# A new table for the order and the engine of every operation in a one-core attention and gMLP kernel

## The chip, the cores and the metric

The kernel runs on one core of a Trainium2 chip (trn2). The metric is the device time of one execution in microseconds. A core has a matrix engine (TensorE, PE in the rows; its weight loads are PEld), VectorE (DVE), ScalarE (ACT), GpSimd (POOL) and a queue engine (SyncE, SP), on which this kernel issues nearly all its transfers. Each engine works through its own list of instructions in order. It stops where an instruction needs something that another engine or a transfer has not yet delivered, and all that stands behind that instruction on the same engine stops with it.

## The reference, cut to what matters

The input is q, k, v of 4 batches, 8 heads, 768 positions and 64 columns in float32, with the four weights of a gated MLP. Each query sees the keys less than 16 positions away and one summary key for each block of 32 positions (24 of them): the elementwise maximum of the block's keys, with the mean of the block's values as its value, and log(32) added to its score. The softmax runs over both kinds together. The heads side by side make x, 768 rows of 512 for each batch, and that goes through the MLP:

```python
h = np.maximum(x @ w_in, 0.0)            # 512 -> 1024
u, v = (h[..., :512], h[..., 512:])
v_n = (v - mean(v)) / np.sqrt(var(v) + 1e-06)
v_s = np.einsum('ts,bsd->btd', w_spatial, v_n) + b_spatial[None, :, None]   # mixes the 768 positions
return (u * v_s) @ w_out
```

## The kernel before, in words

**Recording and emitting.** The kernel is not written as loops that issue instructions. A first pass (`plan.add`, class `Plan`) records 2194 operations, each with the engines that may run it, a planned duration, the buffers that it reads and writes, and a function that issues its instructions. `Plan.order` then takes the operations one by one out of the table `ORDER`: three characters each, two for the operation's number in base 64 and one for the engine. For each it works out a planned start from fixed durations and assigns a slot to each of the operation's buffers that has none yet. The emission loop after that issues the operations sorted by planned start. So the table sets the order of the instructions on each engine, the engine of each operation that has a choice, and which slot each buffer gets and after whom. Two more things hang on the planned starts. The first is the filler: up to the operation "warm" TensorE gets one small matmul that nobody reads for each 300 ns of planned idle time (L904), 33 of them (two instructions each) before the first scores or weight preparation. The second is that a GpSimd operation planned in the first part of the kernel waits for the last VectorE operation on their common port that was emitted before it:

```python
listed = [(self.ops[LETTERS.index(ORDER[i]) * 64 + LETTERS.index(ORDER[i + 1])], ENGINES[int(ORDER[i + 2])]) for i in range(0, len(ORDER), 3)]
...
op, e = listed[len(made)] if listed else choose()
```

**Transfers.** All loads and stores but the last store are issued on SP's queue (helper `dma`, L267), in the table's order. A load into a slot waits on the queue until the slot's old content has been read, and the later loads wait behind it; no more than 8 transfers are outstanding at once. Buffers have few slots: one for a vT tile (`vt`), two alternating ones for the queries (qd) and for the values (ve), six for the spatial weights (`wl`) and three PSUM banks of the kind `m` for projections and other results.

**Names.** In the text `k0_1` is the load of the keys of batch 0, head pair 1; `q0_1_0` the load of the queries of batch 0, chunk 1 (256 positions), pair group 0; `v0_1_0` and `h0_1_0` the two loads of that group's values into ve; `vt1_0_2` the third quarter of batch 1's transposed values for head pair 0; `vn` the values of batch 0 in their natural layout; `wi1_c` and `wi0_c` the load of row block c of the v half and of the u half of w_in; `tr1_7_0` a reload of spatial weights for product 7 of batch 1, part 0.

**The start.** The weights must be split into a high part, which the matmul takes exactly, and a low part. For each block of w_in (`split64`, L283 to L320) ScalarE scales (L296), VectorE shifts and masks (L297, L298, L301, L305), one of the two casts (`copy`, L273), and TensorE or GpSimd forms the rest (L313 to L315, or L319 and L320). A key tile is prepared by VectorE's maxima over 16 keys (L400), a second maximum (L410) and ScalarE's copy into the key tile (L413). The "first scores" are those of batch 0, chunk 0, group 0, and need two key tiles and one query tile.

**Attention.** A group has 2 head pairs and 256 positions. TensorE computes its scores (s, L491) into PSUM; VectorE adds the mask and takes the maximum (L504), ScalarE exponentiates and sums (L508), VectorE adds a small constant and inverts the sums (L512, L514), and one of three engines normalizes (L519, L521). TensorE transposes (t, L540, L548), ScalarE or VectorE copies the result out as pt, and TensorE multiplies with the values ve (x, L564). x leaves PSUM as a high part xh (L273) and a low part xl (VectorE, L579). The block means of the values of batches 1 to 3 come from vT tiles that VectorE reduces (vs_in, L460).

**MLP.** Every product is three matmuls: high by high, and the two mixed ones (L598). proj v (pv) and proj u (pu) make the halves of h, with ReLU on the way out of PSUM; VectorE and others normalize v's rows (L630 to L646); the spatial products (sp) mix positions, VectorE adds them to sums and bias (L738, L740); a gate multiplies with u (L689), casts to gh (L273) and subtracts for gl (L691); proj out (po) gives the result, which leaves through a copy (ob) and a store. Batch 0 takes w_spatial as it is. For batches 1 to 3 w_spatial's quarters are combined beforehand into sums and differences, so that seven half-size products do for eight; these weights lie in device memory and are read back (tr, 384 KB each) into the six `wl` slots for each product. A reload can start as soon as the last product that reads its slot is done.

The attention of batch 0 (and a part of batch 1) comes first, with little projection work to lay beside it; from about 49 us TensorE has projections of one batch beside the attention of the next.

Of the kernel before, what the change touches and what calls it, by code (L numbers as in the profile page):

```python
# [197 lines left out]
def tile_local_summary_attention_gmlp(ctx: ExitStack, tc: tile.TileContext, qT, kext, vext, vnat, vT, w_in, w_sp, b_rep, w_out, out):  # L198
# [734 lines left out]
    "1P41Q21R11S11x41T11y21z11A11C21B10340810911G41H21I11J11D10240030510610100a21K11L21Y41Z20721+11-12012121E01F22210440b0"  # L933
    "0t10i10u20g10h20r10s20j20z40G30n10o21M10p10q20e10f21U10c10d21V12302410y40H30C40A40D40B40J00N20M20I30W40-10K20F3101112"
    "2O40k10l10V40v10w12P03510L22Q13622U12V22W12R21W02-10m32n42o20x30Y13312S13020Z10+20O00Q00R22p10P23112q12r13222s12u30X4"
    "1X21201711821912T20E41511621312e40S01422w41k11l21g11e12t12v31i11N03j43k05V40T10U11a21b11j25W11c11h26L01f21m11d13Q43a4"
    "1n12x22y11o12X23423712Y12f22g11O23813935X41p01q23n11r01s26z06A03y12543A12Z13B23l13o23w13x23p13C13D23r13e02F42+35Y12h1"
    "2i13z24l43m23s23E12z11t02k18q43q23t13F13G33R03W15Z43u11u23v31v12623b43c03d13f26M02G23H43I41w02j25+13Y13Z24716N02H1271"
    "3L02B12812I14512A12D33M24113X28Y43J03K28z43g03h26343U13i12a23S16O04316P26Q14m04E14622l33V24A14C13N03O26412m34D26R16S1"
    "4223P14c46B06T36C08n42J14824425-43T27702C17807902E14B28C44r16D24F22K13+17a04K42L18w46X08Z22M16Y06Z06+02917b22b14y14z2"  # L940
# [126 lines left out]
```

## Time and profile before

| | us |
|---|---|
| median of 3 runs (397.4 to 401.26) | 397.51 |
| the profiled execution | 399.03 |
| its span in the trace | 397.3 |
| TensorE busy | 380.5 |
| VectorE busy | 296.5 |
| ScalarE busy | 215.5 |
| GpSimd busy | 139.8 |

The mean granted clock of TensorE was 1.00 of full speed. In a row of a timeline the first number is the start within the span, the second the duration; the end of the row in square brackets is the idle time of the engine just before and what ended it. "issue" stands for no releaser that the profile shows. Matmuls are pipelined, so that the durations of neighbours overlap, and a row with a count groups instructions that follow one another.

### The profile page before, as it was taken

The page shows a single profiled execution, that of the slowest core. Times are in us where ns is not written, and L with a number is a line of the kernel's source. Part 1 is how long each engine was busy: PE and PEld are TensorE (multiplying, and loading weights), DVE is VectorE, ACT ScalarE, POOL GpSimd, SP SyncE. Part 2 cuts the span into 40 slices and gives each one's busy share as a digit, 9 for nine tenths or more (in the row PEclk, how much of TensorE's full clock was granted, in tenths as well). Part 3 has the DMA queues.
Part 4 walks back from the last instruction along what each step waited for, and adds up shares of the span by engine and source line. Part 5 has one row for each costly group of instructions (what it writes and reads, how often), then busy time and mean ns, then how long its engine had stood idle before and what let it go on. Part 6 is the DMA issues. An engine that isn't in the chain of part 4 may idle for free.

```text
span 397.3 us, 9692 instructions
## 1 busy us (share of the span) xinstructions
PE 380.5 (96%) x3523; PEld 331.5 (83%) x3523; DVE 296.5 (75%) x999; ACT 215.5 (54%) x703; POOL 139.8 (35%) x156
## 2 busy tenths in 40 slices
PE   8889798999999999997989999999999999999996
PEld 8667686899989888897978888899987888898985
DVE  4979798899998979978696586785697667463631
ACT  4779696588484684555448557265447482120110
POOL 4234406412345446661033034443441144310330
PEclk9999999999999999999999999999999999999999
DMA  7978789765366899798925696448961380059304
GB/s 284 395 187 241 193 274 259 217 205 167 133 199 231 298 266 309 240 296 297 357 91 170 197 330 159 127 121 267 298 209 24 105 272 7 2 184 316 148 1 159
DMA packets 41407, 81.77 MB, mean 206 GB/s; under 512 B 4496, under 2 KB 16272, under 8 KB 41360
## 3 DMA queue, kind: packets, MB, share of 16 engines
q1 hardware_dynamic: 41216, 81.02, 64.1%
q8 instruction: 28, 0.46, 0.5%
q14 instruction: 19, 0.16, 0.1%
q10 hardware_dynamic: 144, 0.13, 0.1%
HBM read 66.58 MB, written 14.55 MB: 204 GB/s over the span
## 4 chain that ended last, share of the span: by engine, by line
PE 76%; DVE 11%; DMA 8%; ACT 2%; issue 1%; SPq 1%; POOL 0%; ACTq 0%; DVEq 0%; POOLq 0%
PE sp L598 17%; PE pu L598 16%; PE pv L598 15%; PE po L598 15%; PE x L564 4%; PE s L491 3%; DVE p L504 3%; DMA tr<-mixed_w 3%; PE warm L904 3%; PE t L548 2%; DMA wi<-in_w_in_dram 2%; DMA wo<-in_w_out_dram 1%; DMA k<-in_kext_dram 1%; DVE gh L273 1%; DMA out_dram<-ob 1%
## 5 line engine op out<-in xcount | busy, mean ns | idle before, releaser
L508 ACT ACTIVATE p<-p,sums 128x120 f32<-128x120 f32 x192 | 73.8, 388 | 37.9 <-DVE sums L504 37.7
L504 DVE CUSTOM_DVE_ANT_0 p<-s,mask 128x120 f32<-128x120 f32 x192 | 44.9, 275 | 11.2 <-PE s L491 11.0
L598 PE MATMUL pu<-xh,win_h 128*128 128x512 f32 (+1 forms) x128 | 43.6, 341 | 0.0
L598 PE MATMUL pu<-xh,win_l 128*128 128x512 f32 (+1 forms) x128 | 43.1, 336 | 0.0
L598 PE MATMUL pu<-xl,win_h 128*128 128x512 f32 (+1 forms) x128 | 43.0, 336 | 0.0
L598 PE MATMUL po<-wo_h,gh 128*128 128x512 f32 (+1 forms) x100 | 38.8, 388 | 1.9 <-DVE xl L579 1.7
L598 PE MATMUL pv<-win_h,xh 128*128 128x512 f32 x96 | 38.8, 404 | 0.0
L598 PE MATMUL po<-wo_l,gh 128*128 128x512 f32 (+1 forms) x100 | 38.2, 382 | 0.0
L598 PE MATMUL po<-wo_h,gl 128*128 128x512 f32 (+1 forms) x100 | 38.2, 382 | 0.0
L598 PE MATMUL sp<-tr,vnh 128*128 128x384 f32 x144 | 37.6, 342 | 0.3 <-DMA tr<-mixed_w 0.2
L598 PE MATMUL pv<-win_l,xh 128*128 128x512 f32 x96 | 37.5, 391 | 0.0
L598 PE MATMUL pv<-win_h,xl 128*128 128x512 f32 x96 | 37.5, 390 | 0.0
L508 ACT ACTIVATION_READ_ACCUMULATOR p<-p,sums 128x1 f32 x192 | 36.5, 190 | 0.0
L277 ACT ACTIVATE u<-pu 128x384 f32<-128x384 f32 (+2 forms) x39 | 13.8, 379 | 41.7 <-PE pu L598 41.7
L598 PE MATMUL sp<-tr,vs 128*128 128x384 f32 x162 | 30.7, 339 | 2.1 <-DMA tr<-mixed_w 1.4
L519 ACT ACTIVATE p<-p,sums 128x120 f32<-128x120 f32 x92 | 28.2, 383 | 7.4 <-DVE sums L514 6.4
L521 POOL TENSOR_TENSOR p<-p,sums 128x480 f32<-128x480 f32 x16 | 15.7, 989 | 43.3 <-DVE sums L514 27.9
L598 PEld LDWEIGHTS sp<-tr,vs 128*128 128x128 f32 x162 | 27.8, 188 | 3.1 <-DVE sums L514 1.7
L564 PEld LDWEIGHTS x<-pt,ve 120*64 120x64 f32 x768 | 23.7, 138 | 7.8 <-issue 4.3
L564 PE MATMUL x<-pt,ve 120*64 120x64 f32 x768 | 25.7, 224 | 3.4 <-issue 1.6
L273 ACT COPY pt<-t 120x512 f32<-120x512 f32 x37 | 20.5, 589 | 12.1 <-PE t L548 9.9
L598 PEld LDWEIGHTS sp<-tr,vnh 128*128 128x128 f32 x144 | 25.3, 188 | 2.0 <-DMA tr<-mixed_w 0.9
(175 smaller groups left out, 931.8 us busy)
## 6 DMA issues: line engine op xcount, KB each, us to landing
tr<-mixed_w SPq DMA_DIRECT2D x36, 384.0 KB, 4.8
tr<-plain SPq DMA_DIRECT2D x27, 384.0 KB, 5.1
k<-in_kext_dram SPq DMA_DIRECT2D x16, 544.0 KB, 6.1
qd<-in_qT_dram SPq DMA_DIRECT2D x24, 256.0 KB, 4.3
ve<-in_vext_dram SPq DMA_DIRECT2D x23, 256.0 KB, 4.7
out_dram<-ob SPq DMA_DIRECT2D x23, 256.0 KB, 3.4
vt<-in_vT_dram SPq DMA_DIRECT2D x48, 96.0 KB, 2.7
wi<-in_w_in_dram SPq DMA_DIRECT2D x7, 512.0 KB, 6.8
```

The costliest lines, as they stand in the source:

```text
L273: (nc.scalar.copy if e == "ACT" else nc.vector.tensor_copy)(out=out_, in_=in_)
L277: nc.scalar.activation(out=out_, in_=in_, func=AF.Relu)
L491: nc.tensor.matmul(out=ps.t[r * QB:(r + 1) * QB, a, i * KW:(i + 1) * KW], lhsT=qt[hs, r, i], rhs=kts[r].t[hs, g * SEG:g * SEG + KW], start ...
L504: add(("DVE", 203), lambda e, i=i, mi=mi: nc.vector.tensor_tensor_reduce(out=pt.t[:, i, :], in0=ps.t[:, a, i * KW:(i + 1) * KW], in1=mask[ ...
L508: add(("ACT", 380), lambda e, i=i: nc.scalar.activation(out=pt.t[:, i, :], in_=pt.t[:, i, :], func=AF.Exp, scale=-1.0, bias=st.t[:, 0, i:i ...
L519: nc.scalar.mul(out=pt.t[:, i, :], in_=pt.t[:, i, :], mul=st.t[:, 0, i:i + 1])
L521: eng(e).tensor_tensor(out=pt.t, in0=pt.t, in1=st.t[:, 0, :BPU].unsqueeze(2).broadcast_to([P, BPU, KW]), op=ALU.mult)
L548: nc.tensor.transpose(out=ps.t[:KW, r, a * CH + i * QB:a * CH + (i + 1) * QB], in_=pts[a].t[hs, i, :], identity=ident[hs, hs])
L564: nc.tensor.matmul(out=ps.t[a * D:(a + 1) * D, r, n * QB:(n + 1) * QB], lhsT=win(buf, n, o), rhs=rhs(n, a, r), start=True, stop=True)
L598: nc.tensor.matmul(out=ps.t[:, :n], lhsT=x, rhs=y, start=(j == i == 0), stop=(j == last and i == 2))
L904: nc.tensor.matmul(out=warm.t[:, :KW], lhsT=ident, rhs=ident[:, :KW], start=True, stop=True)
```

## The change

Only the strings of `ORDER` differ, all 62 rows of them; no constant, no function and no operation is different. Decoded, both tables list the same 2194 operations: 551 on TensorE, 280 transfers on SP, and 1363 on the other three. 211 operations have another engine: 58 go from VectorE to ScalarE, 49 from ScalarE to VectorE, 55 from GpSimd to VectorE, 39 from VectorE to GpSimd, 6 from GpSimd to ScalarE and 4 from ScalarE to GpSimd. VectorE then has 798 operations (791 before), ScalarE 452 (441), GpSimd 113 (131).

```diff
@@ -930,63 +930,63 @@
 ENGINES = ("PE", "DVE", "ACT", "POOL", "SP")
 LETTERS = "0123456789abcdefghijklmnopqrstuvwxyzABCDEFGHIJKLMNOPQRSTUVWXYZ+-"
 ORDER = (
-    "1P41Q21R11S11x41T11y21z11A11C21B10340810911G41H21I11J11D10240030510610100a21K11L21Y41Z20721+11-12012121E01F22210440b0"
-    "0t10i10u20g10h20r10s20j20z40G30n10o21M10p10q20e10f21U10c10d21V12302410y40H30C40A40D40B40J00N20M20I30W40-10K20F3101112"
-    "2O40k10l10V40v10w12P03510L22Q13622U12V22W12R21W02-10m32n42o20x30Y13312S13020Z10+20O00Q00R22p10P23112q12r13222s12u30X4"
...
-    "x+0x-2xP1xQ4yd0ye0yf0yg0yh2y04")
+    "0030340810911Y41Z21+11-12122010a20240510611G41H21I10720101J12210440b00r10p10e11x41y20f20c10g10h20d21P41Q21z11K10t11A1"
+    "1C20n10B40o21B12300i11D11E00j22w42x21R11S12y10k12O42P02z11T10z40u20A40q20s20v10l10m31L21F20D42411U23113222U12V22W12X2"
+    "1M12S10w13312Q12T22R20O00P20G30y40C40V40J02-13510x30Q00M20K20Y10F30Z12Y12Z10+20R20W40-12n42o20H32A11011121V10L20N22p1"
...
+    "y04y90ya0yd0ye0yb2yc4yf0yg0yh2")
```

The places of which the prediction speaks, decoded from both tables (list of one engine, in order):

```
SP, from the first transfer
  before: wi1_2 wi1_0 k0_1 wi1_1 k0_0 wi1_3 q0_0_0 vn1 vn0 vn4 vn2 vn5 vn3 k0_3 q0_1_0 k0_2 wi0_2 q0_0_1 h0_0
  after:  k0_1 wi1_3 k0_0 wi1_1 q0_0_0 wi1_0 wi1_2 vn3 wi0_3 q0_1_0 vn1 vn2 vn5 vn0 vn4 k0_2 k0_3 wi0_2 q0_0_1
SP, transfers 28 to 33
  before: wi0_3_256 q0_2_1 ws1 vt1_0_2 h0_1_0 v0_1_1
  after:  ws5 h0_1_0 vt1_0_2 wi0_3_256 v0_1_1 q0_2_1
PE, first operations
  before: wi1_0 (rest) s0_0_0 wi1_3 (rest) vs s0_1_0 wi1_2 (rest) t0_0_0
  after:  s0_0_0 wi1_3 (rest) wi1_0 (rest) s0_1_0 t0_0_0 vs t0_0_0
DVE: reduce of vt1_0_2: place 94 before, 99 after
PE: the four steps of pu1_1_0: places 205, 212, 221, 222 before; 231 to 234 after, between sp1_2 and sp1_6
```

## Rows read from the trace of the kernel before

**Rows 1.** The page, part 1: busy time of each engine.

```profile
PE 380.5 (96%) x3523; PEld 331.5 (83%) x3523; DVE 296.5 (75%) x999; ACT 215.5 (54%) x703; POOL 139.8 (35%) x156
```

**Rows 2.** Windows: length; busy PE, PEld, DVE, ACT, POOL; clock; DMA share; GB/s.

```profile
...
13.80:49.00 35.20, 29.30 (x460) 22.86 (x460) 30.24 (x148) 29.09 (x105) 14.33 (x16) 1.00 0.83 240
49.00:85.00 36.00, 34.39 (x292) 29.07 (x291) 32.88 (x119) 26.70 (x80) 12.78 (x12) 1.00 0.81 241
85.00:175.00 90.00, 89.90 (x859) 79.24 (x859) 78.19 (x267) 56.70 (x195) 42.84 (x44) 1.00 0.75 236
175.00:188.00 13.00, 10.90 (x62) 10.12 (x61) 11.18 (x31) 6.80 (x28) 4.00 (x3) 1.00 0.85 272
188.00:208.00 20.00, 18.29 (x235) 17.13 (x235) 16.05 (x45) 8.73 (x24) 3.40 (x2) 1.00 0.67 231
208.00:360.00 152.00, 151.78 (x1363) 131.16 (x1362) 105.14 (x355) 77.67 (x261) 50.07 (x50) 1.00 0.53 167
...
```

**Rows 3.** TensorE's timeline: start, duration, line, operation, count, idle before and releaser.

```profile
2.29 10.25 PE L904 MATMUL warm<-ident 128*128 128x120 f32 x66
...
13.80 1.05 PE L491 MATMUL s<-k,qd 64*64 64x120 f32 x32
...
19.96 1.05 PE L491 MATMUL s<-k,qd 64*64 64x120 f32 x32 [1.70 <-DMA qd<-in_qT_dram]
...
26.32 1.05 PE L491 MATMUL s<-k,qd 64*64 64x120 f32 x32 [1.61 <-ACT k L413]
...
42.99 1.15 PE L564 MATMUL x<-pt,ve 120*64 120x64 f32 x32 [1.46 <-DMA ve<-in_vext_dram]
...
64.37 0.82 PE L564 MATMUL x<-pt,ve 120*64 120x64 f32 x21 [1.61 <-issue]
...
182.93 3.42 PE L598 MATMUL sp<-tr,vs 128*128 128x384 f32 x18 [0.62 <-DVE f L740]
187.79 0.95 PE L598 MATMUL sp<-tr,vs 128*128 128x384 f32 x4 [1.45 <-DMA tr<-mixed_w]
...
207.68 0.47 PE L598 MATMUL po<-wo_h,gh 128*128 128x512 f32 x1 [1.71 <-DVE xl L579]
```

**Rows 4.** ScalarE's timeline.

```profile
4.77 0.67 ACT L296 ACTIVATE wi<-wi 128x512 f32<-128x512 f32 x1 [2.71 <-DMA wi<-in_w_in_dram]
...
11.79 0.68 ACT L296 ACTIVATE wi<-wi 128x512 f32<-128x512 f32 x1 [0.25 <-DMA wi<-in_w_in_dram]
12.69 0.43 ACT L413 COPY k<-gm 128x288 f32<-128x288 f32 x1 [0.21 <-DVE gm L410]
...
43.08 0.40 ACT L508 ACTIVATE p<-p,sums 128x120 f32<-128x120 f32 x1 [2.64 <-DVE sums L504]
```

**Rows 5.** VectorE's timeline.

```profile
8.53 0.95 DVE L400 TENSOR_REDUCE gm<-k 128x48 f32<-128x768 f32 x1
...
42.44 0.35 DVE L460 TENSOR_REDUCE vs_in<-vt 128x6 f32<-128x192 f32 x1 [2.11 <-DMA vt<-in_vT_dram]
...
200.84 1.85 DVE L273 CAST gh<-f 128x384 fp32r<-128x384 f32 x1
...
206.85 0.68 DVE L579 TENSOR_TENSOR xl<-x,xh 128x512 fp32r<-128x512 f32 x1
```

**Rows 6.** SP's timeline: issues of transfers.

```profile
14.91 0.33 SPq L267 DMA_DIRECT2D qd<-in_qT_dram  x1
...
35.87 0.33 SPq L267 DMA_DIRECT2D vt<-in_vT_dram  x1
36.24 1.91 SPq L267 DMA_DIRECT2D ve<-in_vext_dram  x3
...
181.99 3.14 SPq L267 DMA_DIRECT2D tr<-mixed_w  x4
```

**Rows 7.** The page, part 6: issues, KB each, median us to landing.

```profile
tr<-mixed_w SPq DMA_DIRECT2D x36, 384.0 KB, 4.8
```

**Rows 8.** GpSimd's timeline.

```profile
200.28 2.20 POOL L691 TENSOR_TENSOR gl<-h,gh 128x768 fp32r<-128x768 f32 x1 [14.23 <-ACT gh L273]
```

More of the change, by code (lines that the diff above doesn't have):

```diff
@@ L937 @@
[L937 to L940, printed above, removed]
@@ new lines @@
+    "0T10U11o31r01s21b11c12542621d13r16L05X43711p02s13816M03n16z03A11q22f23933e05Y12B23l13m23w13y13C13z23c02712g13s23p12h1"
+    "2812j13x23o21t02i11u22u31v13Q43R04713S14116A04516B03a43q23t16C03W13u18C43B23D23E13F13d23f23b44315Z45+13g02F42G23G23v3"
+    "3Y14623H43U13V23J03K22k13h13i13L03M22l32H14l44m02m12916D22I16E14424p13I43N03O23P14824n18Y42a28t44A14B22v34226341w0641"
+    "2D36N06O02c12K22b12J14918Z23Z25042M17707807907a04S46F12C12E15-43X23T23+16P24a16X06Y06Z06+02L12N33-14029e49f24d44e04E1"
@@ new lines @@
+    "4F24r14s22d38D27j04y14z26G16H37k04f24t16016Q17b14C14o28w48x26R16S19547l07m06147c17d17o27v07w07x04D27y04b14V16T36U18+1"
+    "8-19g14W19014u24q24v16214G14H17n26V26W34w14x24-45215314g07p07q07e14h29216I14c48y14L04i08n46-28o18p34I24N06J24j24M24O2"
+    "5427017114J44K49127r07s07t26b44k16c18E18z48A27f37u29334T45515618B34U44P04Q24R17215727336545147B06614Y14Z18u27C07D09h1"
+    "4+24X28q48r29n49417g17h27H07I08P47J07K09i16K16746819F47L27417528s19625805m15o19G29O45p29o27A16947635K15915v15n25w27M1"
@@ new lines @@
+    "6a1ct45k17T07U07V07W05I18v38F45x17z27E07X28805f15G15H27F27Y17Z17+18i06d47G18G45z15l25J25q18j07N18k08l08m27O17i37-3801"
+    "8129p19R48908a06e18b08c1cu47P38Q28d08e07Q17R25a28218308408508608728f08g09q18h29s27S1as08R1a806f46g15M15b15y29r19u15r2"
+    "9Y45A29H18S18T15L2at0au0av05c25d1aw0ax09+09S48H29t19715g2a90aa0ab06h45N26i19v18I1ay1ai0aj0ak0al0981am05B19k19Q45C25O1"
+    "5P15D15E16j49w46k15e25h15i19-0a00a105s18J18K19I1an09j15t15R45Q29x28L29919a25j39b16l46m1a205S4a308U25u25F29J16u06x26v2"
@@ new lines @@
+    "ac09X49K28M1ao18N18O19l15T46n4a416o1ad06p0ap36t26s29c36r26q26y16w1az3aA2ae15U49y19z19A19B19C18V18W18X3fs4bc0aq2ft1bd0"
+    "9L19d1be0bf09P4bg0af1ag2fu4a51a62b209D19E19V4cv0cy2fv1d71d82d01d12db1dc2cE1cF29Z49M3cW1cR1cS2fw4d91da2di49N3cY1cN1cO2"
+    "cL1dg4cz1c+1b30b40b50fx1c-2cC1a73fy49W4b60b70cX2b81bh0cZ2aU0aV0aB3cA1bm0ah19T4d51cM2cB2d62aW0cG1cH2cP1cQ2ar1dd1d21d31"
+    "bi1dq4aX0aY0aZ0de1dh49m3aI0aJ0fz1aK0aL0cD2cI1cJ1cT1cU1a+1d43cK2cV3aO0df2dk0do2dn2b91a-1aM1cw1cx1dj4fC4fD1dm1dp4aP0aQ0"
@@ new lines @@
+    "aR0aS1fA4fB1dl2dr0du2dw1e51dC1in49U4dH1dv1dL1dJ1bn0ds2e11aN4e22dK2dD2bo0bp0bq0br0aT4dS1bj1bk2dI2bl3dM2e71dU1ba2bb3dA1"
+    "dW1fE4fF1ew4dN1dO2dx2aC0aD0aE0dY1dZ2aF0dX2e31dt1e42bs1bt3e62b02dT2gg0gh0gi0gj0aG1dP1bO1g60dQ1dB2em4er1g70eu4g80hk0g90"
+    "ev4eA1gk1dV2bu2ee4fG4b13bv1bC0gl1fH1bD0bE0ga2bP4eB1d+1d-1dy1dz2aH4bQ4dR2gm1gn1es1en4et2go3gp1bR1e82bS1bT3gw2cf4fI4bV2"
+    "el4cg4ef4bF0bG2ex1he0hf0hg0hh0dE1hj2fJ1eC2bU3gA0gb1c14bH4e91ea1e02dF1gc1bZ2dG2ey1eb3ed4gd1hl0ge3hm0bX4eo1ep1ch1ci1cj1"
@@ new lines @@
+    "hn0hp2gf1ec4cl2cn4hi2cm1gq1b+1ck1gB0gC0gD0gr3eg0eh1gu1gv1gE2gF1gG1gH1bw0bx0eq2gs3gt1bW1fK4fL1b-4gK0gL0gM0ek2gN0c24gx1"
+    "c31c43ei2ho2ej2ez2eD0f41f81gy2eX1cp2eM1c04fM4cq3gI3gO2bY4eE2eO1h20eG2eH1h30h40h50c72h62eF1by0bz0hA0hB0eK1bA2co4ki4cr4"
+    "fN1cs4hC0bB4c53gP1gQ1gR1c61cb2fO4gJ1f52f61eT1cc1h71hq0gS3gT1hr0gU1c94gV3gW1gY2fq4fd1fe2hs0ht0gZ3eN2eV1gX3hD0hu1hv1hw1"
+    "cd4fP1c81hx1hy3hZ0hE2h+0h-0g+2i00i12hF1h80h90ie4ha0hG1hH1eU2hb0eP2fh1hd2bI0bJ0eW2i70hz1hI3hJ1hc2hK1hL1hO1ce4hP1ic4gz1"
```

78 lines of the change are left out of this document (29 added, 49 removed).

## The prediction

> **What bounds the kernel now.** I read the page's busy times first, then the busy time of each engine in eight stretches of the span, then TensorE's timeline with what ended each idle gap, and last the timelines of the engines that those gaps name. TensorE is busy for 380.5 of 397.3 us [rows 1]; the reader should see there that only its idle time and the start can be won, since the change leaves its 551 planned operations the same. The stretches say where that idle time lies: 85 to 175 has 0.10 us of it and 208 to 360 has 0.22, so no reordering can gain there; 13.8 to 49 has 5.90, 49 to 85 has 1.61, 175 to 188 has 2.10 and 188 to 208 has 1.71 [rows 2]. Before 13.8 nearly all of TensorE's work is filler (the 66 filler matmuls of 10.25 us), and the first scores start at 13.80 [rows 3]. The single gaps are few: 1.70 before the second scores (a q load), 1.61 before the third (a key), 1.46 before the x at 42.99 (a ve load), 1.61 at 64.37, 0.62 at 182.93 (VectorE's add of a spatial sum), 1.45 at 187.79 (a spatial weight read back), 1.71 at 207.68 (VectorE's xl) [rows 3]. So this is a TensorE kernel with about 11 us of stalls in six places and a late start. I go through the places that the new table changes.
>
> **A, the start.** The old table loads four parts of w_in among the first six transfers and the first q seventh. Their landings can be seen on ScalarE, whose first scale waits until 4.77 for load one and whose fourth starts at 11.79 on load six [rows 4]: 7.0 us for five loads, 1.40 us each of about half a MB. The new table has k0_1, a w_in part, k0_0, a w_in part, q0_0_0: so k0_1 at 4.8, k0_0 at 7.6, the fourth load at 9.0, q (half the size) at 9.7. Behind k0_0 come a key reduce on VectorE, 0.95 [rows 5], a small maximum, then ScalarE's copy into the key, 0.43 [rows 4], but ScalarE has the scale of the fourth load ahead of that copy (9.0 to 9.7). So scores one start at about 10.2, not 13.80: 3.5 us earlier. The filler is counted by the plan's idle time up to its first operation; that operation is planned earlier too, so the filler gets shorter and doesn't hold the scores. Most of the 3.5 is given back at once, because w_in preparation that the old table had done by then (two parts; the scale alone is 0.67 of ScalarE [rows 4]) is still ahead of the softmax or between its pieces. q0_1_0 waits for scores one on the load queue; it was issued at 14.91 [rows 6] and is now issued at about 11.3, but the other v and key loads, formerly before it, are now behind it. Through the keys of the third scores I get 24.8 for it instead of 26.32 [rows 3]: **-1.5**. Bounds: +0.6 (rival three) and -3.5 (all of it kept).
>
> **B, 40 to 43 us.** VectorE takes its list in order. At 42.44 it reduces a vT tile for which it has waited 2.11 us [rows 5]; that load could be issued only at 35.87, when the single vt buffer was free, and the ve load that the x at 42.99 needs was issued behind it at 36.24 [rows 6]. Queued behind the reduce are softmax masks; ScalarE's exponentials wait 2.64 for them [rows 4]. The new table puts the ve load ahead of vt1_0_2 and the reduce five places further back on VectorE, behind masks. The x then needs only its pt, and the masks don't wait. Worth at least the 1.46 that TensorE loses [rows 3], at most the 2.64 that ScalarE loses. I take 2.5, nearer to the upper end, since the dense projections start only once this chain of masks and exponentials is through: with A **-4.0** at about 49 us.
>
> **C, 49 to 85.** Here VectorE is busy 32.88 of 36 us and TensorE 34.39 [rows 2]. The engines of 211 operations change; counted here they give VectorE some 1.1 us more. Its idle 3.1 us take some of that, so the cost lies between 0 and 1.1; taken +0.5. Of the 1.61 at 64.37 [rows 3] the new order fills only a little (one transpose goes ahead of that x, and its copy waits on the same VectorE): -0.4, bounds 0 and -1.6. Front so far **-3.9**; what is late next is VectorE's layernorm before the first spatial products.
>
> **D, 85 to 175:** 0.10 us idle [rows 2], nothing to win; covers are over a long stretch of work queued on TensorE.
>
> **E, 182 to 188.** The spatial weights of batches 1 to 3 are read back into six slots. A reload can start when the products that read the slot are through, and it must land before the products of the next one; the TensorE work between is its window. The new table moves four small steps of proj u (pu1_1_0, each three matmuls of 256 columns) into that window, between the steps sp1_2 and sp1_6. Eighteen sp matmuls of 384 columns took 3.42, or 0.19 each [rows 3]; scaled to 256 columns twelve take 1.5. The 0.62 and the 1.45 make 2.07, all between those same points, so about 0.6 is left: **-1.4**. Bounds: -2.1 if the reload comes no later than without the gap; +1.0 if the vt load ahead of it in the load queue, which waits for its buffer, is itself later (the reloads behind it were issued from 181.99 on [rows 6]).
>
> The median landing of such a reload is 4.8 us after its issue [rows 7]. The Trainium skill, "DMA: Bandwidth & Descriptors", section "Anatomy of one DMA", has about 2 us fixed and 436 GB/s: an estimate by that page is 2.9 us for 384 KB, by which every window here would do and the sum would be 1 us lower. The trace's median disagrees for these queued trains, so the sum goes by the trace.
>
> **F, 200 to 208.** VectorE casts gates itself: 1.85 us [rows 5] while POOL runs a 2.20 us subtraction [rows 8]. Masks and then the xl of x2_0_1 queue behind, until 206.85 + 0.68 [rows 5]; only that frees the PSUM slot for which TensorE waits 1.71 at 207.68 [rows 3]. In the new table some of these gates' multiplications go to POOL and casts to ScalarE, and the xl comes sooner in VectorE's list. Of 1.71 I take **-1.0**; POOL's train is longer now and po then waits for it. Bounds -1.7 and +1.0 (one more POOL piece of about 1 us, half of that 2.20).
>
> The Trainium skill, "SBUF — State Buffer", section "SBUF: two separate sides", says that VectorE and GpSimd share a port pair under an exclusive lock, and the loser fully blocks. The 1.85 us cast beside the 2.20 us subtraction agrees.
>
> **G, later reloads.** In batches 2 and 3 the new table has windows, counted in the sp steps of three matmuls (0.19 each [rows 3]) between, of 3.7 us for one slot and 4.2 to 4.7 for five more, against the 4.8 median [rows 7]; the old has five of 4.0 to 4.7, and yet lost only 0.22 in 208 to 360 [rows 2]. Nearest row for a late one is the 1.45. **+0.6**, bounds 0 and +2. **H, waits not seen now:** a new order has its own small ones, in size between the 0.10 and 0.22 of the dense stretches and one gap of 1.6: **+0.9**, bounds 0 and +2. The tail keeps its order but for one output copy on another engine, hidden by the matmuls of the last projection up to its end: 0, and at most that copy, about half a us, if it comes last.
>
> **Sum:** -3.9 - 1.4 - 1.0 + 0.6 + 0.9 = -4.8. The profiled execution took 399.03, 1.5 above the median of 397.51; against it 394.2, and against the median **392.7**.
>
> **Rivals.** One: the front's gain is eaten in 49 to 85. VectorE, 91% busy there [rows 2], sets when sp0 starts, and its added 1.1 us plus waits that only moved take back all of A and B. Then E and F with G and H are left: 397.5 - 0.9 = 396.6, and with a sixth of the front kept **396**. For it: VectorE's busy share; against: at 42.44 VectorE itself waits 2.11, so B starts VectorE earlier too. Two: each stall that goes is replaced by one elsewhere: 397.5. For it: neighbours change places on every engine, and reload windows get tight; against: the gaps have single causes that the order removes. That nothing changes at all is no rival: the table is read operation by operation, so the order is done as written. Three, slower: the load queue blocks at its head. q0_1_0 is tenth and waits for scores one; five v loads, k0_2, k0_3 and q0_0_1 stand behind it. If scores one start later than about 12.5 (ScalarE late with the key's copy), those land as much later as in the old order and in a longer train: the third scores at about 28.7, +2.4 on 26.32 [rows 3], B's gain is lost because its loads come late too, and the time is 397.5 + 2.4 + 0.5 (C) - 2.4 (E and F) + 1.5 (G and H) = **399.5**. For it: the same wait is seen now, where the q load is issued at 14.91 [rows 6], when scores one of 13.80 have taken their 1.05 [rows 3]. Against: the first key and q lead the queue.
>
> The Trainium skill, "DMA: Bandwidth & Descriptors", section "Anatomy of one DMA", says that DMA engines don't wait on semaphores, the issuing sequencer does; the q load issued at 14.91 agrees.
>
> **How the numbers follow.** Forecast case 0.52, its own range 390 to 395 from the bounds of C, E, F and G; rival one 0.27, two 0.11, three 0.10. The range 389.5 to 398.8 leaves out rival three and the far ends of the sum. Changes within 1% (4 us) can't be told from none: faster takes most of the forecast case, 0.48; slower by more than 4 us needs rival three with G's upper end or E's, 0.10; the rest 0.42.
>
> **What would show it.** A: first scores near 10.2, third near 24.8. B: no VectorE wait on a vt load and no TensorE wait on ve near 40; projections of v about 4 us earlier. C: gap at 64 shrunk little, first sp about 3.9 earlier. E: one gap of about 0.6 in place of two. F: a po wait under 0.8 that no longer names xl. G: sp waiting for tr in batches 2 and 3, under 1 us in all. It is wrong if the first dense spatial product comes less than 2 us earlier, or if tr waits in the later batches exceed 2 us.

## The result: 392.89 us after 398.14, by another road than forecast

| | before | changed |
|---|---|---|
| median of four runs each | 398.14 (397.4 to 401.26) | 392.89 (391.32 to 396.22) |
| the same again, later (17 and 6 runs) | 398.17 (394.66 to 400.17) | 392.89 (391.7 to 393.49) |
| profiled execution, its span | 399.03, 397.3 | 393.65, 391.9 |

The ratio is 0.9854 with an interval of 0.9812 to 0.9896, and 0.9854 (0.9827 to 0.9881) the second time: 1.5% faster, 5.3 us. Ratios and ranges leave out runs more than 1.5% above the fastest of their kernel; medians leave out none. The forecast was 392.7, a drop of 4.8 from the 397.51 known then; beside the changed kernel the kernel before measured 398.14.

The page's busy times of the changed kernel, and its windows over the same times as [rows 2] (length; busy PE, PEld, DVE, ACT, POOL; clock; DMA share; GB/s):

```profile
PE 381.4 (97%) x3517; PEld 330.9 (84%) x3517; DVE 296.3 (76%) x1006; ACT 220.5 (56%) x705; POOL 117.5 (30%) x138
```

```profile
13.80:49.00 35.20, 32.23 (x441) 24.66 (x440) 31.64 (x141) 31.50 (x109) 12.84 (x14) 0.95 0.81 259
49.00:85.00 36.00, 36.00 (x304) 31.11 (x303) 34.36 (x130) 31.95 (x102) 15.25 (x15) 1.00 0.80 251
85.00:175.00 90.00, 89.22 (x850) 77.82 (x849) 76.34 (x261) 56.95 (x184) 30.47 (x33) 1.00 0.75 236
175.00:188.00 13.00, 12.98 (x104) 12.30 (x103) 10.45 (x29) 5.87 (x19) 4.64 (x3) 1.00 0.92 299
188.00:208.00 20.00, 19.81 (x210) 17.62 (x209) 15.65 (x57) 9.81 (x37) 8.55 (x7) 1.00 0.71 236
208.00:360.00 152.00, 151.09 (x1370) 131.18 (x1369) 105.93 (x348) 74.66 (x239) 36.85 (x37) 1.00 0.54 169
```

The stretches that had gaps are full now: 49 to 85 has none left (1.61 before), 175 to 188 has 0.02 (2.10) and 188 to 208 has 0.19 (1.71). The dense ones lost a little: 0.78 idle from 85 to 175 (0.10), 0.91 from 208 to 360 (0.22). From 13.8 to 49 TensorE is busier by 2.9 us, but the granted clock is 0.95 there: a part of that busy time is slow work, not more work.

TensorE's timeline of the changed kernel, the lines that answer to [rows 3]:

```profile
10.85 1.05 PE L491 MATMUL s<-k,qd 64*64 64x120 f32 x32 [0.86 <-ACT k L413]
...
17.46 1.05 PE L491 MATMUL s<-k,qd 64*64 64x120 f32 x32 [0.71 <-DMA qd<-in_qT_dram]
...
26.40 1.31 PE L491 MATMUL s<-k,qd 64*64 64x120 f32 x32 [1.97 <-ACT k L413]
27.65 2.07 PE L313 MATMUL wwi<-wi,ident 128*128 128x512 f32 x2
...
41.57 1.15 PE L564 MATMUL x<-pt,ve 120*64 120x64 f32 x32
...
61.41 0.80 PE L564 MATMUL x<-pt,ve 120*64 120x64 f32 x20
...
189.72 0.61 PE L598 MATMUL sp<-tr,vnh 128*128 128x384 f32 x2 [0.17 <-DMA tr<-mixed_w]
...
202.17 0.44 PE L598 MATMUL po<-wo_h,gh 128*128 128x512 f32 x1
...
235.70 1.15 PE L548 MATMUL t<-ident,p 64*120 64x64 f32 x32 [0.76 <-DVE p L521]
```

The gaps before the x at 42.99, at 64.37, 187.79 and 207.68 are gone. Those before the second and the third scores stay (0.71 and 1.97), and a new one of 0.76 stands at 235.7. The third scores start at 26.40, where they stood at 26.32.

**One profile of each is too little here.** The kernel before ran from 394.66 to 402.12 us over the runs of this study, and one and the same wait on a load differs by over 1 us between profiles (the one ahead of the x at 42.99 [rows 3]: 0.19 to 1.46 in the five that have the old order there). Some experiments below take one part of the table from the old order and the rest from the new one; where the two parts meet there is a seam. Whatever such a run leaves as it was is one more sample of the old or the new order. So I cut TensorE's list at places where both orders have done the same operations, and took the length of each stretch (from the start of the Nth planned operation to that of the next mark) in every profile in which that stretch and what leads to it have the one order or the other, without a seam inside:

| TensorE's operations | old order: median (range), profiles | new order: median (range), profiles | difference | forecast |
|---|---|---|---|---|
| start to 33rd | 47.2 (46.7 to 48.9), 5 | 47.7 (47.0 to 52.4), 5 | +0.5 | A and B -4.0 |
| 33rd to 72nd | 29.3 (28.9 to 30.0), 6 | 28.4 (28.2 to 29.0), 7 | -0.9 | C, +0.1 |
| 72nd to 144th | 44.7 (44.6 to 45.1), 5 | 45.0 (44.5 to 45.4), 7 | +0.3 | with C |
| 144th to 191st | 35.2 (35.2 to 35.4), 4 | 36.2 (35.6 to 36.5), 6 | +1.0 | H |
| 191st to 253rd | 34.9 (34.6 to 35.6), 4 | 33.1 (32.7 to 33.7), 6 | -1.8 | E -1.4 |
| 253rd to 268th | 13.18 (13.17 to 13.21), 4 | 11.31 (11.30 to 11.34), 8 | -1.9 | F -1.0 |
| 268th to 382nd | 77.3 (76.7 to 77.5), 4 | 78.1 (77.0 to 79.0), 7 | +0.8 | H |
| 382nd to 503rd | 84.9 (83.6 to 85.5), 6 | 82.7 (82.7 to 83.0), 8 | -2.2 | G +0.6 |
| 503rd to the end | 26.7 (26.7 to 27.3), 6 | 26.8 (26.6 to 27.2), 8 | +0.2 | 0 |

H was 0.9 for all stretches together. "The end" is that of the issue of the last store. The medians sum to -4.1 of the 5.3 measured; with so few profiles of a front that varies by 2 us and more they can't do better, and where the other 1.2 us lie stays open. What they do show of the gain lies behind the 191st operation (157 us), not in the front.

### The profile page after: what moved, and what is told of

It is laid out like the page before. It is cut to its first block, busy times and chain, and to the rows that moved or that the text cites. A ratio compares the mean times of both kernels' runs of the same rounds, so it can differ in the third digit from the quotient of the medians.

```text
span 391.9 us, 9657 instructions
## 1 busy us (share of the span) xinstructions
PE 381.4 (97%) x3517; PEld 330.9 (84%) x3517; DVE 296.3 (76%) x1006; ACT 220.5 (56%) x705; POOL 117.5 (30%) x138
## 4 chain that ended last, share of the span: by engine, by line
PE 78%; DMA 12%; DVE 6%; ACT 2%; issue 1%; SPq 0%; DVEq 0%
PE sp L598 19%; PE pv L598 15%; PE pu L598 15%; PE po L598 13%; PE x L564 6%; PE s L491 5%; DMA vt<-in_vT_dram 5%; DMA wi<-in_w_in_dram 3%; DMA tr<-mixed_w 3%; PE t L548 2%; DVE p L504 2%; DMA qd<-in_qT_dram 1%; PE t L540 1%; DVE xl L579 1%; DVE vs_in L460 1%
## 5 line engine op out<-in xcount | busy, mean ns | idle before, releaser
L508 ACT ACTIVATE p<-p,sums 128x120 f32<-128x120 f32 x192 | 73.9, 387 | 29.8 <-DVE sums L504 29.5
L598 PE MATMUL sp<-tr,vnh 128*128 128x384 f32 x144 | 37.6, 342 | 0.4 <-DMA tr<-mixed_w 0.2
L633 POOL TENSOR_TENSOR mv<-mv,mhalf 128x1 f32<-128x1 f32 x24 | 13.8, 577 | 63.4 <-DVE mv L632 59.9
L521 POOL TENSOR_TENSOR p<-p,sums 128x480 f32<-128x480 f32 x16 | 16.2, 1017 | 50.4 <-DVE sums L514 20.9
L519 ACT ACTIVATE p<-p,sums 128x120 f32<-128x120 f32 x80 | 24.7, 383 | 5.1 <-DVE sums L514 4.4
L491 PE MATMUL s<-k,qd 64*64 64x120 f32 x768 | 23.4, 267 | 3.5 <-ACT k L413 2.8
```

The source lines that it names most:

```text
L491: nc.tensor.matmul(out=ps.t[r * QB:(r + 1) * QB, a, i * KW:(i + 1) * KW], lhsT=qt[hs, r, i], rhs=kts[r].t[hs, g * SEG:g * SEG + KW], start ...
L508: add(("ACT", 380), lambda e, i=i: nc.scalar.activation(out=pt.t[:, i, :], in_=pt.t[:, i, :], func=AF.Exp, scale=-1.0, bias=st.t[:, 0, i:i ...
L519: nc.scalar.mul(out=pt.t[:, i, :], in_=pt.t[:, i, :], mul=st.t[:, 0, i:i + 1])
L521: eng(e).tensor_tensor(out=pt.t, in0=pt.t, in1=st.t[:, 0, :BPU].unsqueeze(2).broadcast_to([P, BPU, KW]), op=ALU.mult)
L598: nc.tensor.matmul(out=ps.t[:, :n], lhsT=x, rhs=y, start=(j == i == 0), stop=(j == last and i == 2))
L633: add(("POOL", 560), lambda e: nc.gpsimd.tensor_tensor(out=mv.t[:, 1:2], in0=mv.t[:, 1:2], in1=mhalf, op=ALU.pow), pri, w=[mv])
```

## The experiments

All edits are to the table; they are given as the lists of one engine, decoded. Times are medians; a ratio is to the kernel before, measured beside the run. e4, e8 and e12 are set against the changed kernel by these ratios (0.9854 for the changed kernel).

**e1 and e2: one half of the change.** One table up to TensorE's 72nd operation, the other one behind it.

```diff
 e1: -old[:72]  +new[:72]   old order for the rest
 e2:  old[:72]  new order for the rest (-old[72:] +new[72:])
```

> The new table up to TensorE's 72nd operation (the first step of proj u of batch 0's last chunk, at 78.9 us in the kernel before and 75.9 in the changed one), the old table for what is left. Both have done the same TensorE work at that point, and there the changed kernel is 2.96 us ahead. Theory (the gains arise where the waits go, and add up): 398.1 - 3.0 = 395.1, and the old gaps near 183, 188 and 208 us are there again. Rival (a lead at the front is given back, since VectorE or the loads set the start of the spatial products): 397 to 398.

> The reverse: the old table up to TensorE's 72nd operation, the new one after it. Theory (gains add up): the changed kernel wins 2.3 to 2.7 us after that point, so 395.5 to 395.8, with no wait on a reload near 188 and none on xl near 208. Rival (the later gain was only the front's lead, which let transfers be early): 397 to 398, with gaps near 188 and 208.

Measured: e1 398.46, ratio 0.9993 (0.9962 to 1.0024); e2 398.17, ratio 0.998 (0.9951 to 1.0009). Neither half gains anything that this can tell, and both theories of e1 and e2 can't hold at once. TensorE's timelines around 80 us, e1 and then e2, show why:

```profile
76.29 0.39 PE L598 MATMUL pu<-xh,win_h 128*128 128x256 f32 x1 [0.87 <-ACT u L277]
...
83.72 0.45 PE L598 MATMUL sp<-wsp_h,vnh 128*128 128x384 f32 x1 [1.29 <-ACT u L277]
```

```profile
81.72 0.39 PE L598 MATMUL pu<-xh,win_h 128*128 128x256 f32 x1 [2.31 <-ACT u L277]
```

Waits on ScalarE's ReLU that the profile of neither kernel has: 2.16 us in e1 and 2.31 in e2, within 8 us behind the seam (the first of e1's is not the seam's alone: e4 and e12 have 0.32 and 0.61 there). The likely reason is that the other engines' lists are cut at a point that fits TensorE's place in one table and not in the other. Of the three old gaps that e1 was to show again, the one on VectorE's add (0.70) and the one before proj out (1.68) are there and the one on a reload is not; e2 has none of the three, as expected. The times say nothing on the halves; their stretches away from the seam are in the table above.

**e5 and e6: the same with the seam at the 191st operation**, inside a long dense run.

```diff
 e5: -old[:191] +new[:191]   old order for the rest
 e6:  old[:191] new order for the rest (-old[191:] +new[191:])
```

> The new table up to TensorE's 191st operation (157 us in the changed kernel, 159 before; TensorE has run without gaps for 70 us there, and the other engines have slack, so the seam should cost nothing), the old table for the rest. Theory (each gain stays where it arises): 1.7 us faster than the kernel before, near 396.8, with the wait on xl near 206 us again and TensorE's stretch from the 253rd to the 268th operation 13.2 us long as before. Rival (the front is worth nothing, as in the run cut at the 72nd operation): 398 to 398.5. Rival (the front is worth all): 394 or less.

> The old table up to TensorE's 191st operation, the new one for the rest. Theory: the rest is worth the larger part, 3.7 us: near 394.8; stretches of TensorE from the 191st to the 235th, the 253rd to the 268th, the 382nd to the 397th and the 440th to the 503rd operation are shorter by about 0.8, 1.9, 0.4 to 1.4 and 0.8. Rival (the later stretches are short only because the front delivers early): 397 or more.

Measured: e5 401.33, ratio 1.007 (1.0032 to 1.0108); e6 401.17, ratio 1.0065 (1.0032 to 1.0098). Both slower than either table. That the seam would cost nothing was wrong again: e6's timeline has

```profile
158.91 0.50 PE L598 MATMUL pv<-win_h,xh 128*128 128x512 f32 x1 [1.12 <-ACT xh L273]
161.83 0.79 PE L598 MATMUL pv<-win_h,xl 128*128 128x512 f32 x1 [2.19 <-DVE xl L579]
```

and its window of those times (columns as above) has a clock of 0.86:

```profile
150.00:175.00 25.00, 21.70 (x199) 17.53 (x198) 21.61 (x63) 8.88 (x24) 8.82 (x10) 0.86 0.76 247
```

In e5 TensorE waits 0.54, 0.61 and 0.75 for ScalarE and VectorE between 171 and 186 us, and the stretch from the 191st to the 235th operation takes 26.4 where the old order takes 23.6 to 24.1.

Just behind the seam e6's first stretch failed the expectation: 28.1 from the 191st to the 235th, where 0.8 less than the old 24.0 was expected. Further on the stretches came out as expected, and that is the part of the expectation that stands: the 253rd to the 268th operation took 13.19 in e5 and 11.33 in e6, the 382nd to the 397th 11.84 and 11.46, the 440th to the 503rd 37.6 and 37.05. So these later gains do not need the new front.

**e3: step B alone**, on the kernel before.

```diff
 SP:  -vt1_0_2 h0_1_0
      +h0_1_0 vt1_0_2
 DVE: -vm1_0_2 m m wi0_3_256 wi0_0_0 wi0_3_0 wi0_0_0
      +m m wi0_3_256 wi0_0_0 wi0_3_0 wi0_0_0 vm1_0_2
```

> The kernel before with one thing of the change alone: the ve load of batch 0, chunk 1 stands ahead of vt1_0_2 on the load queue, and VectorE's reduce of that tile comes seven places later in its list. The prediction's step B: VectorE's 2.11 us wait and TensorE's 1.46 us wait at 43 us go, and it is 2.5 us faster (bounds 1.5 and 2.6), 395.6. Rival (the next thing is late as well: the masks, exponentials and copies behind make the same x late): under 0.5 us, 397.7 to 398.1.

Measured: 397.81, ratio 0.9953 (0.9921 to 0.9986): 1.9 us faster by the ratio (0.6 to 3.1), 1.0 by the medians (398.85 before). VectorE's and TensorE's timelines of e3, against [rows 5] and [rows 3]:

```profile
42.29 0.35 DVE L460 TENSOR_REDUCE vs_in<-vt 128x6 f32<-128x192 f32 x1
```

```profile
41.63 1.15 PE L564 MATMUL x<-pt,ve 120*64 120x64 f32 x32
```

Both waits are gone. They belong to the old order: its four other profiles have the one on vt at 0.59 to 2.01 us and the one on ve at 0.19 to 1.41, and no profile of the new one has either. From the third scores to this x it is 15.1 us in e3 and 15.4 to 16.7 (median 16.2) in the five old ones, so about 1.1 is won up to there. Step B's mechanism is shown; its size is 1 to 2 us, and the 2.5 of the forecast lies within the interval. The rival (under 0.5 us) is refuted for this order. In the changed kernel the x comes at 41.57, no earlier than with B alone, and no earlier than in the median of the five old profiles, 41.59.

**e4: the second q behind the v loads**, on the changed kernel: is it the blocked queue that ate step A?

```diff
 SP: -q0_1_0 vn1 vn2 vn5 vn0 vn4 k0_2
     +vn1 vn2 vn5 vn0 vn4 q0_1_0 k0_2
```

> The changed kernel with the second q load five places later on the load queue, behind the five loads of v that wait behind it now (it waits for the first scores, until 11.96 us, and no transfer lands between 14.2 and 17.4). Theory (the head of the queue blocks, and that ate step A): the keys of the third scores land some 2.5 us earlier, those scores start at about 24.2 in place of 26.4, TensorE's idle 2.0 us before them goes and with it the fall of the clock after it (1.5 us): 2 to 3 us faster than the changed kernel, 390 to 391. Rival (ScalarE's order is the cause: the scale of a w_in part ahead of the key's copy): third scores still 26 or later, 392.5 to 393. Second rival (the second q is then late itself, its scores 1 us later): 393 or more.

Measured: 394.27, ratio 0.9893 (0.9845 to 0.994): not faster than the changed kernel. The second q is now late itself (e4, TensorE), as the second rival had it, and the third scores start at 26.34:

```profile
19.57 1.05 PE L491 MATMUL s<-k,qd 64*64 64x120 f32 x32 [2.77 <-DMA qd<-in_qT_dram]
```

TensorE does not idle before the third scores in this profile, and its granted clock is 1.00 from 13.8 to 49 us, as the theory had it; the time is no shorter for it.

**e8: the third q and the key's copy ahead of a w_in part**, on the changed kernel.

```diff
 SP:  -wi0_2 q0_0_1
      +q0_0_1 wi0_2
 ACT: -wi0_2 (scale) p0_3 (key copy) vs1 vs3
      +p0_3 (key copy) vs1 vs3 wi0_2 (scale)
 DVE: three steps of wi0_2 from before to behind the masks of s0_0_1,
      a fourth of them six places further back
```

> The changed kernel, where a part of w_in (wi0_2) is loaded just behind the third q instead of ahead of it, and its scale on ScalarE comes behind the copy of the last key and two copies of value sums (its first three steps on VectorE behind the masks of the third scores). Theory (ScalarE's order at 25 us, where it waits 1.03 us for that load with the key's copy queued behind, is what holds the third scores): they start near 25.2 in place of 26.4, TensorE's idle 2.0 us before them is under 1, its clock does not fall, and the dense run starts 1 to 2.5 us earlier: 390.5 to 392. Rival (the stream of loads and VectorE's list bound the stretch as a whole, so that what is taken ahead is missing later): third scores earlier, but the dense run starts within 0.5 us of the changed kernel's: 392.5 to 393.5.

Measured: 393.74, ratio 0.984 (0.9794 to 0.9886), beside 0.9854 for the changed kernel: no difference that this can tell. TensorE's timeline of e8:

```profile
24.55 1.04 PE L491 MATMUL s<-k,qd 64*64 64x120 f32 x30 [0.16 <-ACT k L413]
...
27.27 1.15 PE L564 MATMUL x<-pt,ve 120*64 120x64 f32 x32
29.72 1.05 PE L491 MATMUL s<-k,qd 64*64 64x120 f32 x32 [0.88 <-DMA qd<-in_qT_dram]
```

The third scores come 1.8 us earlier and the first x 3.2 earlier (30.50 in the changed kernel), as the theory had it, and the clock stays at 1.00. So the load and the scale of wi0_2 did hold the third scores. But the next x is only 0.5 earlier (36.69 after 37.24), and the 33rd operation starts at 47.1 us, 0.5 before the changed kernel's 47.7: what was taken ahead was missing behind. That is the rival's sign. It fits a front that is bound as a whole, by its loads and by the lists of ScalarE (31.50 us busy of 35.20 in the window above) and VectorE (31.64), and not by one wait; no run separates the three.

**e11: filler ahead of the third scores**, on the changed kernel, for the clock. In the changed kernel the weight preparation at 27.65 took 2.07 for its first two matmuls, where it took 1.13 at 20.94 and 1.02 to 1.13 elsewhere: near half the rate. The granted clock is 0.50 there, 1.2 in place of 2.4 GHz, from 27.3 to 30.7 us, after an idle time of 1.97.

```diff
+            if op.tag == "s0_0_1":
+                for _ in range(6):
+                    nc.tensor.matmul(out=warm.t[:, :KW], lhsT=ident, rhs=ident[:, :KW], start=True, stop=True)
             idle = op.end
```

> The changed kernel with six more filler matmuls (1.8 us) ahead of the third scores, where TensorE idles 1.97 us and its clock then falls. Theory (the fall costs time of its own, beside the wait): no fall after that gap, the block of weight preparation behind it takes 1.4 us in place of 2.85, and the time is 1 to 1.5 us under the changed kernel's. Rival (the chain from there on runs through ScalarE's exponentials and VectorE, so that a slow TensorE there costs nothing): the same time within 0.5 us.

Measured: 393.82, ratio 0.9898 (0.9866 to 0.9931): not faster, if anything slower than the changed kernel's 392.89 beside it (e10). The clock did stay up (e11, TensorE):

```profile
24.41 1.50 PE L907 MATMUL warm<-ident 128*128 128x120 f32 x12
26.67 1.17 PE L491 MATMUL s<-k,qd 64*64 64x120 f32 x32 [0.75 <-ACT k L413]
27.77 1.13 PE L313 MATMUL wwi<-wi,ident 128*128 128x512 f32 x2
```

The matmuls at half speed cost nothing that the times show. That is the rival; that the work waited for ScalarE and VectorE in any case is its reason, not measured by itself. A granted clock below 1.00 in a window is not yet a loss.

**e7 and e9: step F alone**, on the kernel before, in two parts: first the casts only, then all that the changed kernel does with that gate.

```diff
 e7: se1_3_1 casts (gh)          -DVE +ACT
 e9: se1_3_1 casts (gh)          -DVE +ACT
     se1_3_1 two multiplications -DVE +POOL
     se1_3_1 subtraction (gl)    -DVE +POOL
```

> The kernel before with two engine letters changed: the casts of the last two gates before proj out of batch 1 (gh, 1.85 and 1.06 us on VectorE at 200.8 and 203.2) go to ScalarE, which idles 4.94 us there. Step F alone. Theory: xl of x2_0_1 comes some 2 us earlier, TensorE's 1.71 us wait at 207.7 goes, the stretch from the 253rd to the 268th operation is 11.3 to 11.5 us in place of 13.2, and the time is 1.7 to 1.9 us shorter, near 396.7. Rival (xh, which stands behind exponentials on ScalarE, is next): the wait shrinks by under 0.5, 398.

> The kernel before with step F as the changed kernel has it: of the gate se1_3_1 (half of f before proj out of batch 1) two multiplications and a subtraction go from VectorE to GpSimd, behind GpSimd's 2 us subtraction, and both casts from VectorE to ScalarE. Theory (what cost the time is VectorE's work on the same memory port beside GpSimd's long subtraction: with the casts on ScalarE, a multiplication took 2.17 us in the cast's place): VectorE goes straight on to masks, which read PSUM and were not slowed beside GpSimd; xl comes some 2 us earlier, no wait before proj out, the stretch from the 253rd to the 268th operation is 11.3 to 11.6 us and the whole 1.6 to 1.9 shorter. Rival (xl behind nine masks is late in any case): 12.5 us as with the casts alone. Second rival (GpSimd's train of five pieces is late for proj out): the stretch is short, but the wait turns up within the next 15 us.

Measured: e7 398.58, ratio 0.9998 (0.9965 to 1.003), and the stretch from the 253rd to the 268th operation 12.53 in place of 13.18. Nothing won that the times can tell, though ScalarE was free and the wait on xl shrank from 1.71 to 0.49. VectorE and GpSimd of e7:

```profile
197.79 2.65 DVE L689 TENSOR_TENSOR f<-f,u 128x384 f32<-128x384 f32 x2
201.02 0.70 DVE L691 TENSOR_TENSOR gl<-f,gh 128x384 fp32r<-128x384 f32 x1 [0.58 <-ACT gh L273]
```

```profile
197.82 2.20 POOL L691 TENSOR_TENSOR gl<-h,gh 128x768 fp32r<-128x768 f32 x1 [13.66 <-ACT gh L273]
199.99 1.32 POOL L691 TENSOR_TENSOR gl<-f,gh 128x384 fp32r<-128x384 f32 x1
```

Two multiplications of 0.55 took 2.65: the second one now stands beside GpSimd's 2.20 us subtraction as the cast did [rows 5, 8], and ends 0.4 us after it (200.44 and 200.02). The cast was not slow; whatever VectorE does next on that memory is. In the changed kernel a cast of the same size, with GpSimd idle, took 0.36:

```profile
203.61 0.36 DVE L273 CAST gh<-w 128x384 fp32r<-128x384 f32 x1
```

This is the exclusive lock that the prediction cited from the Trainium skill, "SBUF — State Buffer", section "SBUF: two separate sides": the trace agrees, and it speaks for the price of the old order, where I had it as a side remark.

e9: 396.09, ratio 0.9941 (0.9909 to 0.9972): 2.3 us faster by the ratio (1.1 to 3.6), 2.1 by the medians (398.17 before), the stretch 11.49, no wait ahead of proj out. GpSimd and, at the same time, VectorE in e9:

```profile
197.26 1.82 POOL L691 TENSOR_TENSOR gl<-h,gh 128x768 fp32r<-128x768 f32 x1 [13.34 <-ACT gh L273]
199.04 1.98 POOL L689 TENSOR_TENSOR f<-f,u 128x384 f32<-128x384 f32 x2
200.97 2.13 POOL L691 TENSOR_TENSOR gl<-f,gh 128x384 fp32r<-128x384 f32 x2
```

```profile
199.01 0.28 DVE L504 CUSTOM_DVE_ANT_0 p<-s,mask 128x120 f32<-128x120 f32 x1 [1.88 <-PE s L491]
```

GpSimd works for 5.8 us on end, and VectorE's masks beside it, which read the scores from PSUM, take the 0.28 that they take anywhere. The theory of the port is shown for this place. A train of five GpSimd pieces was not late for proj out.

The gain is that of the twelve runs; the profiled one, 398.78, is among the longest of them. In it the transposes of the last attention groups of batch 2 wait for GpSimd's normalizing, and the clock falls behind that wait (granted 0.79 from 236 to 244 us; e9, TensorE):

```profile
238.61 0.69 PE L548 MATMUL t<-ident,p 64*120 64x64 f32 x16 [1.61 <-POOL p L521]
```

The stretch from the 268th to the 382nd operation took 79.4, where the old order takes 76.7 to 77.5. Two other profiles with the old order there (e1, e5) wait 0.44 and 0.57 at this place; whether step F makes the wait longer, one profile does not tell.

**e10: the changed kernel once more.**

> The changed kernel itself once more, for its time beside the others of this call and a second trace. The forecast's 392.7; from its first four runs (391.3 to 396.2) 392 to 395. Stretches of TensorE that are the change's doing come out again as in its first trace (253rd to 268th 11.30 us, 382nd to 397th 11.43, 440th to 503rd 37.05 to 37.4); stretches that are chance (up to the 33rd, 235th to 241st) vary by 1 us or more.

Measured: 392.89 (391.7 to 393.49). The 253rd to the 268th operation took 11.34 us, the 382nd to the 397th 11.43, the 440th to the 503rd 37.05, as in the first trace; the clock fell at the same place. The two stretches that I expected to vary by 1 us or more did not: 47.55 after 47.69 up to the 33rd, and 3.13 both times from the 235th to the 241st. The latter took 3.13 in all new orders, and 3.23 to 3.44 in e1, e3, e5, e7 and e9, which have the old order there, but 4.87 in the one profile that I had: the wait of 1.45 at 187.79 [rows 3] was chance in its place and size. A smaller one for the same reloads stands a few steps on in e3, e7 and e9, 0.79, 0.43 and 0.49 in all up to the 253rd (0.1 at most in e1 and e5). The longest (e3, TensorE):

```profile
189.15 0.62 PE L598 MATMUL sp<-tr,vnh 128*128 128x384 f32 x2 [0.61 <-DMA tr<-mixed_w]
```

**e12: the transposes at 235 us behind two steps of proj v**, on the changed kernel, the one leftover wait that looked cheap.

```diff
 PE: -t2_2_0 pv2_2#0 pv2_2#1
     +pv2_2#0 pv2_2#1 t2_2_0
```

> The changed kernel with one step moved: TensorE's transposes of the last attention groups of batch 2 (t2_2_0), which wait 0.76 to 1.3 us near 235 us for VectorE's normalized probabilities, come two steps of proj v (1.36 us) later. Theory (the wait is covered by work that was ready): no such wait, 0.7 to 1.3 us faster than the changed kernel, 391.6 to 392.2 beside its 392.9. Rival (what the transposes feed is then late by as much: the scores behind them, their softmax or the x): the same time, and a wait at s3_0_0 or the next x.

Measured: 395.59, ratio 0.992 (0.9885 to 0.9955): slower than the changed kernel. The wait at the transposes is gone, and a longer one stands at the step that was moved ahead (e12, TensorE), since its PSUM bank is freed by an output copy on ScalarE:

```profile
238.43 0.50 PE L598 MATMUL pv<-win_h,xh 128*128 128x512 f32 x1 [2.09 <-ACT ob L273]
```

The stretch from the 287th to the 315th operation took 22.4 in place of 20.7 and 21.4. The work that "was ready" was ready only because the transposes came first. No version here beats the changed kernel by more than the noise.

## Why the prediction came out right, step by step

The total was right, to 0.2 us, and so were the sign and the range (the drop was 5.25 in place of 4.8, from a start that measured 0.6 higher); its distribution was not. It had 3.9 us of the gain in the front and 0.9 behind; the table above has about 0.1 in the front (start to 144th) and 4.0 behind.

- **A, failed.** The step was right for the first scores (10.85 measured, 10.2 forecast) and wrong for the third: 24.8 forecast, 26.40 and 26.24 in two traces of the changed kernel. I followed the keys, gave the loads that stand behind the blocked q a bound (rival three), and left out the third q and the w_in part ahead of it. The changed kernel's load queue (SP), ScalarE's list there and TensorE in the second trace (e10) show what bound it:

```profile
11.96 0.33 SPq L267 DMA_DIRECT2D qd<-in_qT_dram  x1
12.33 2.54 SPq L267 DMA_DIRECT2D vn<-in_vnat_dram  x5
14.92 1.66 SPq L267 DMA_DIRECT2D k<-in_kext_dram  x2
```

```profile
25.25 0.66 ACT L296 ACTIVATE wi<-wi 128x512 f32<-128x512 f32 x1 [1.03 <-DMA wi<-in_w_in_dram]
25.81 0.42 ACT L413 COPY k<-gm 128x288 f32<-128x288 f32 x1
```

```profile
26.24 1.22 PE L491 MATMUL s<-k,qd 64*64 64x120 f32 x32 [1.86 <-DMA qd<-in_qT_dram]
```

The second q is issued at 11.96, near the 11.3 of the forecast; but the keys, issued from 14.92 on, have five v loads and the stream ahead, and their copy stands behind a scale that waits for yet another load. The third q comes behind that same load and releases the third scores in e10 (so too in e1, e5 and e12, whose front is the new one). What these scores need was loaded no earlier, with one more part of w_in ahead of it. With wi0_2 behind both (e8) they start at 24.55, near the 24.8 of the forecast; but e4 and e8 show that neither the blocked q nor this load alone was the bound of the front.
- **B, mechanism right, size 1 to 2 in place of 2.5** (e3). That A and B together make 4.0 at about 49 us failed: the front up to the 33rd operation is no shorter than before in the median, and the projections of v, forecast about 4 us earlier, start at 33.47 after 31.13. The prediction had named its own test: wrong if the first dense spatial product comes less than 2 us earlier. In the two profiles first compared it came 3.0 earlier (84.62 and 81.66). But three more traces with the old order up to there have it at 82.45 to 82.78, and three more with the new one at 81.92, 84.29 (e12) and 86.89 (e5): the first profile of the old order was a late one, and the new order varies by 5 us there. Over the four traces of each the medians are 82.7 and 83.1, so by that test the front's part of the forecast is wrong.
- **C, the balance right, the parts not.** The gap at 64.37 went whole (in new orders no wait there, in five old ones 0.6 to 1.6), where I left 1.2 of it; in e3, which has step B alone, it is 0.23, so it may hang on B; VectorE's added work, which I priced at 0.5, shows as nothing: TensorE has no idle time from 49 to 85 while VectorE is busy 34.36 of 36. -0.9 up to the 72nd operation, in place of +0.1.
- **E, right in sum, one size by chance.** -1.8 in place of -1.4. Of the 2.07 that I counted, the 0.62 on VectorE's add is a true cost of the old order (0.38 to 0.75 in all six of its profiles), and no new order has it. The 1.45 is mostly chance: the waits on reloads from there to the 253rd operation come to 0.4 to 0.8 in e3, e7 and e9 and to 0.36 at most in the new orders. Together the idle time is some 1.1 shorter; the other 0.7 is not idle time, and its cause stays open. No run moved the four steps alone.
- **F, mechanism right, mis-sized:** -1.9 in place of -1.0, and -1.7 with F alone (e9). I kept 0.7 for a GpSimd train that would be late for proj out; it wasn't.
- **G, wrong sign:** +0.6 forecast, -2.2 measured. The old order loses on reloads in batches 2 and 3, 0.6 to 1.8 us in four of six traces, but only 0.3 in the one I had (0.2 in e5). TensorE of e9 and of e3 there:

```profile
284.85 3.75 PE L598 MATMUL sp<-tr,vs 128*128 128x384 f32 x18 [1.20 <-DMA tr<-plain]
```

```profile
362.18 0.62 PE L598 MATMUL sp<-tr,vnh 128*128 128x384 f32 x2 [0.91 <-DMA tr<-mixed_w]
```

The new order takes 82.65 to 83.01 over that stretch in eight traces, with 0.06 idle at most; the old one idles 0.2 to 1.9 (median 1.4, of it up to 0.7 for VectorE's sums), and some 0.7 of the difference is not idle time. The cause stays open: by the prediction's own count the new windows are no wider (3.7 to 4.7 us in place of 4.0 to 4.7), so the windows alone don't explain it, and no experiment changed them. The 2.9 us that the prediction set beside the 4.8 is an estimate for another path: the Trainium skill, "DMA: Bandwidth & Descriptors", section "Anatomy of one DMA", gives its fixed time and rate for transfers issued from GpSimd, and these reloads are issued on SP.
- **H, too small:** 0.9 forecast, 1.0 and 0.8 measured in two stretches. From the 144th to the 191st operation waits under 0.4 us each come to 0.0 to 0.6 (median 0.3); the rest of the 1.0 is not idle time and not explained. From the 268th to the 382nd it is the wait of the transposes at 235 to 243 us (0.70 to 1.34 in five of seven traces) or one on a reload (1.15 in e4).
- **Two slips that changed nothing.** The gaps that the prediction lists are seven and sum to 10.2 us, where it speaks of about 11 in six places; and its 66 filler matmuls are 33 of two instructions each.
- **Rivals.** One (the front's gain is eaten, about 396) was right about the front and wrong about the time, since E, F and G gave more than I allowed. Two and three did not come.

So the agreement to 0.2 us is largely luck: an error of +3.8 in the front met one of -3.1 behind. F and one wait of E were on the list with their causes; the gain of G was not on it, and which stalls belong to the order and which to the run, one profile did not tell.

## What to carry to other kernels

Before a stall from one trace goes into a sum, ask whether another run of the same program has it: here single waits on transfers came and went by about 1 us, while the stretch with the wait on VectorE's xl repeated to 0.04 (13.17 to 13.21). Take over an order as a whole or change single neighbours: half a table cost 2 us and more at the seam in all four tries. And a stall that went in a stretch where three engines are over 85% busy (13.8 to 49) was mostly found again further on.

## What the runs showed of the hardware that I had not expected

- A two-input VectorE operation on 384 columns takes 0.55 us alone and over 2 us (2.65 for two of them) beside a GpSimd subtraction of 2.20, and ends 0.4 after it (e7); a cast of that size takes 0.36 alone and 1.85 beside one. Masks that read PSUM take 0.28 beside 5.8 us of GpSimd work (e9).
- In the changed kernel TensorE ran at half its clock for 3.4 us (27.3 to 30.7, granted 0.50) behind 1.97 us of idle time; six filler matmuls kept it up, and the kernel was no faster. The idle time alone does not tell whether the clock falls: it did not in e1 behind 1.90 and in e4 behind 2.77 (granted 1.00 from 13.8 to 49).
- The same program varies by some 2% between runs (394.66 to 402.12). Among the profiles, stretches of one order differ most up to the 33rd operation (46.7 to 48.9 old, 47.0 to 52.4 new) and, in the old order, where reloads are waited for (83.6 to 85.5 from the 382nd to the 503rd).
